# Packing the first segment's score visits into 512 columns, in a kernel whose instruction order is a searched list

## The chip, the cores and the metric

The kernel runs on one core of one Trainium2 chip. The metric is the device time of one execution in microseconds, from the program's start to its end; lower is better. Five engines work side by side, each in its own order of instructions: TensorE (PE, with PEld for its weight loads), VectorE (DVE), ScalarE (ACT), GpSimd (POOL) and SyncE (SP, which here only issues DMAs). They wait for each other through semaphores.

## The reference, cut to what matters

A pre-norm transformer block in bf16: 2048 tokens, 640 columns, 32 heads of 20. The attention is Infini-attention, over 4 segments of 512 tokens, with a memory (M, z) carried from segment to segment. The MLP has 1728 hidden columns.

```python
def _A_ref(x, wq, wk, wv, wo, beta):          # B=1, S=2048, H=32, Dh=20, N=4 segments, L=512
    ...                                       # q, k, v = x @ w, split into heads and segments
    phi = lambda t: jnp.where(t > 0, t + 1.0, jnp.exp(t))
    g = sigmoid(beta)
    for s in range(N):
        logits = jnp.einsum('bhqd,bhkd->bhqk', qs, ks) * scale + mask     # causal
        a_dot = softmax(logits) @ vs
        num, den = phi(qs) @ M, phi(qs) @ z + 1e-06
        o = g * num / den + (1.0 - g) * a_dot
        M, z = M + phi(ks).T @ vs, z + phi(ks).sum()
    return o @ wo
h  = x + _A_ref(layernorm(x), wq, wk, wv, wo, beta)
h2 = h + silu(layernorm(h) @ w1) @ w2
```

## The kernel before, in words

**Order.** Every piece of work is a task with a name. A string, `ORDER`, lists all tasks in the order in which they are recorded; each engine runs its own tasks in that order. The part of a row behind `:` gives the buffers (PSUM banks among them), the part behind `/` another engine than the task's first choice (`/A` ScalarE, `/D` VectorE, `/G` GpSimd). `fillN` are N matmuls on zeroes, put where TensorE is expected to have nothing else.

**Front of a segment** (`declare_front`). Blocks of 128 tokens are normalised: statistics (`n1_st`, DVE), the reciprocal root (`n1_r`, POOL, its first step in some blocks on DVE), the scaling (`n1_ap`, DVE, into `xn_rot`). The result is turned to columns by a DMA transpose (`n1_tr`, on SP's queue) in segments 1 to 3. In segment 0 TensorE turns it (`n1_tp`, line 750) and one copy of 640 columns a block brings it from PSUM to `hT` (`n1_te`, lines 759 and 760). The weights wq and wk are loaded raw into `sT` and rearranged by copies (`re_wq`, `re_wk`) into five chunks of 128 columns: each chunk holds four heads in strips of 32 partitions, 20 rows a head; the 12 rows left over hold pieces of the last 12 heads. Projections (`pr`, line 826) make q (w=0) and k (w=1) of chunk c; in segment 0 each is made in two halves of 256 tokens, x and y (`pr040x`: segment 0, chunk 4, q, first half), and copied out by `qe`. `v` (line 793) makes v, copied out by `ve`.

**The gathered tile.** The last 12 heads' q and k are put together from the left-over rows by 12 DMAs (`vt`, line 845, on SP's queue), into three more chunks, groups 5, 6 and 7. Before them the tile is zeroed by one memset (`vz0` for segment 0, `vz1` for the tile of the later segments, line 847). In segment 0 these tiles lie in the memory of w2 (`w_sb` in the profile).

**Score visits** (`scores`). For a group g of four heads, `qk` (line 912) makes the causal score blocks, keys on partitions and queries on columns, into four PSUM banks, one a head; two ScalarE instructions (`e`, line 923) take the exponential of two banks each into a slot of `PT`; POOL zeroes the upper triangle of each diagonal block (`mk`, line 934). In segment 0 a group has three visits: `x`, queries 0 to 255, 384 columns (256 for key block 0, 128 for key block 1); `ya`, queries 256 to 511 with key blocks 0 and 1, 512 columns; `yb`, the same queries with key blocks 2 and 3, 384 columns.

**Tick** (`tick`). `av` (line 955) multiplies by v, `oe` (lines 968, 970) copies out, `tn` turns the result back, `nm` normalises it into `otok`. `kt`, `mz`, `ma`, `mb` make the memory: `kt` is a DMA transpose of phi(k).

**Back** (`declare_back`). `ot` turns `otok` by a DMA transpose on SP's queue, `wo` (line 1124) multiplies by wo, `rs` adds the input; `n2_...` normalises and turns again by DMA; `h1` (line 1159), `th`, `s` are the first MLP product with the silu, `h2` (line 1201) the second, `o` and `out` the result. The MLP of one segment is spread between the score visits of the next.

`warm` (line 588) is a tanh of zeroes, 1280 wide, that writes two spare rows of `w2_sb` before the last rows of w2 are loaded over half of each.

Of the kernel before, what the change touches and what calls it, by code (L numbers as in the profile page):

```python
# [324 lines left out]
D = 640  # L325
# [3 lines left out]
L = 512  # L329
# [24 lines left out]
epsc:0 zpad x0:0 iota sel halfc x1:1 w_q:0 vz1:0 n1_st0:5 x2:2,3 n1_st1:3 n1_r0 n1_r1/D warm:0 n1_ap0:0 n1_ap1:1  # L354
fill29:7 n1_tp0:0 n1_te0:0 re_wq2:0 re_wq3 n1_st2:7 fill3:2 n1_tp1:2 w_k n1_r2 n1_te1 n1_st3:0 re_wq0/A fill8:4
pr020x:4 re_wq1/A re_wk0:0 pr030x:5 re_wq4 re_wk1/A mt0 n1_ap2:2 pr000x:6 re_wk2 pr010x:7 n1_r3 n1_ap3:3 pr001x:0
qe000x:0 re_wk3 pr011x:1 qe020x:0 n1_tp2:2 x8:4,5,6,10 qe010x:0 n1_tp3:6 qe030x/D:0 re_wk4/A pr021x:4 qe011x n1_te2
qe001x/D pr041x:5 beta qe021x/D x4:7,8,9,11 n1_te3/D w_w1_0:0 n1_st9:1 w_w1_2 qk0x0:0 lsc0 qe041x:0 e0x0:0 e0x2
pr040x:4 pr031x:5 w_wv:0 n1_st7:3 pr041y:6 vz0/G:0 qk1x0:0 n1_r7 qe040x qe041y e1x2:1 lsc1 pr030y:7 pr040y:4 pr031y:6
qe031x/D e1x0 qe040y mk0x_0 w_w1_4 qe031y qk2x0:0 n1_st6:2 e2x2:2 qe030y/D pr011y:5 n1_st4:4 e2x0 pr001y:4 pr000y:7  # L360
n1_r4/D mk1x_0 qk3x0:0 mk2x_0 pr021y:6 qe000y/D qe021y/D vpad1 pr010y:7 n1_st5:6 qe001y/D mk2x_256 e3x2:3 e3x0 qe011y
n1_ap7:0 pr020y:2 vt04 vt08 v00:0 mk1x_256 qe020y vt01 qe010y ex011:0 ex031:1 vpad0 lsc2 qk4x0:2 ve00/D:0 vt011 e4x0:6
n1_r6/D pha011:0 vt05 n1_st8:5 v01:6 mk0x_256 vt02 e4x2 qk0yb0:0 vt06 mta0 ve01/D zf0 phb011 v03:4 pha001:1 mk3x_0
vt03 vt00 n1_r5/D lsc3 pha031:2 ex001:2 mtb0 e0yb0:4 e0yb2 n1_ap4:1 vt07 vt09 n1_ap6:2 av0x:6 av2x:7 n1_r9/D mk4x_0
vt010 n1_ap5:3 qk1yb0:0 ve03 mk3x_256 phb031 v02:4 e1yb2:5 oe0x/D:0 e1yb0 oe2x/D:1 mk4x_256 qk7x0:0 ve02/D e7x2:0 e7x0
n1_tr4:0 tn0x:6 mm1 mm6 n1_tr5 av1x:7 kt01:0 oe1x/D:0 n1_tr6 qk5x0:2 w_w1_3 tn1x:7 av3x:0 e5x0:2 nm0x:0,0 nm1x:1 e5x2
oe3x/D:0 mk7x_0 mk7x_256 tn2x:6 fill3:1 qk6x0:0 av4x:7 av7x:4 e6x2:1 nm2x:2 v11:5 pha051:0 e6x0 oe7x/D:1 phb001 ve11:1
mk0yb_0 n1_tr7 mk6x_0 mk6x_256 tn7x:3 v10:0 mk5x_0 ex051:0 ex021:1 oe4x/D:1 qk0ya0:4 mk5x_256 e0ya0:3 tn3x:2 mk0yb_256
# [35 lines left out]
s0_1_1 pr230:6 th0_0_1:1 s0_0_1 e16e0:4 qe230 ad14 tn15:0 e16e2 mk16b_0 h1_0_10_1:7 h1_0_12_1:2 h1_0_5_1:3 pha200:0
kt16:0 th0_10_1:0 ex220:1 nm15:3,0 ad15 mz16:6 pha201:0 ex200:0 kt17:1 vt210:0 h1_0_6_1:4 ot6:0 s0_10_1 th0_12_1:1 ot7
ex201:2 v22:0 th0_6_1:0 s0_12_1 pha220:0 h1_0_11_1:5 th0_5_1:1 mk16a_0 h1_0_2_1:7 s0_6_1 mz17 ve22 ot4 out1/A s0_5_1
vt22 th0_11_1:0 th0_2_1:1 ot5 qk17b0:0 s0_11_1 e17b0:5 ma13 phb201 s0_2_1 vt28 kt20:1 ex211:2 wo6:4 h1_0_9_1:6 e17b2
mk16b_384 h1_0_3_1:7 mk16e_0 vt25 pha221:2 phb220 rs6 vt21 pha211:1 qk18b0:0 vt27 wo7:4 th0_3_1:0 mk16e_256 e18b0:0
th0_9_1:1 n2_st6:6 e18b2 vt20 phb200 vt23 s0_3_1 av16:0 n2_r6 pha230:0 rs7 ex230:1 ex221:0 s0_9_1 h1_0_13_1:1 qk17a0:2
oe16/D:1 th0_13_1:0 e17a2:1 wo4:6 mk17b_0 e17a0 s0_13_1 phb211 mk17b_384 h2_2_0:0 phb221 rs4 n2_st4:0 qk18e0:4 wo5:2  # L410
# [50 lines left out]
def build(nc, es, A_x, A_wq, A_wk, A_wv, A_wo, A_beta, B_x, B_w1, B_w2, out):  # L461
# [815 lines left out]
```

## Time and profile before

| | |
|---|---|
| time of the runs, median (lowest to highest) | 303.35 us (302.07 to 304.94), 3 runs |
| the profiled execution's own time | 302.65 us |
| its span in the profile | 300.9 us |
| granted TensorE clock | 1.00 throughout |
| PE busy | 288.7 us, 96% |
| DVE busy | 234.4 us, 78% |
| ACT busy | 230.5 us, 77% |
| POOL busy | 135.8 us, 45% |

Busy shares are means over stages with different limits. PE's end times are modelled, with pipelined matmuls laid over each other, so that a busy PE may still lose time in short steps; what ends a stage is seen in the waits of that stage. A row of the timeline gives the start, the length, the engine, the line, what is written and read, how many instructions were merged, and in brackets the engine's idle time just before with what ended it.

### The profile page before, as it was taken

Reading aid. Unit: us, or ns where it says so; the run is one execution under the profiler, and the core shown is the slowest. Engines: PE = TensorE matmul, PEld = TensorE weight load, DVE = VectorE, ACT = ScalarE, POOL = GpSimd, SP = SyncE. Lnnn points to the kernel's source line nnn. Section 1 sums busy time; section 2 is a strip of 40 time slices with the busy share of each in tenths; the row PEclk is TensorE's granted clock in tenths of the full one; section 3 lists DMA queues with packets and bytes.
Section 4 is the critical chain, followed back from the end, with each engine's and each line's share of the span. In section 5 each row is a group of like instructions: output and inputs, shape, how many; then the busy total and the mean of one; then the engine's idle time right before and its main releaser. Section 6 shows DMA issues by size and latency. Waiting matters only on the chain.

```text
span 300.9 us, 7531 instructions
## 1 busy us (share of the span) xinstructions
PE 288.7 (96%) x2994; PEld 169.5 (56%) x2994; DVE 234.4 (78%) x553; ACT 230.5 (77%) x337; POOL 135.8 (45%) x246
## 2 busy tenths in 40 slices
PE   8899888999999999989999899999999999999996
PEld 6675545555555455666643445556564457764575
DVE  6989887878798979879899976967868687835523
ACT  3889898999999999989889979998999741004500
POOL 2537843544566664445746715465395640200000
DMA  7953595556535320253662330233161004130002
GB/s 259 332 183 61 122 202 121 124 144 116 96 72 103 74 59 1 37 119 63 99 164 47 35 68 2 45 70 59 20 89 46 0 2 109 38 96 24 22 22 89
DMA packets 53603, 25.85 MB, mean 86 GB/s; under 512 B 44032, under 2 KB 52480, under 8 KB 53568
## 3 DMA queue, kind: packets, MB, share of 16 engines
q1 hardware_dynamic: 52144, 23.81, 36.5%
q10 hardware_dynamic: 1424, 1.56, 1.5%
q8 instruction: 24, 0.39, 0.6%
q14 instruction: 11, 0.09, 0.1%
HBM read 10.41 MB, written 2.62 MB: 43 GB/s over the span
## 4 chain that ended last, share of the span: by engine, by line
PE 66%; ACT 13%; DVE 12%; DMA 5%; issue 2%; POOL 1%
PE ps_all L1201 18%; PE ps_all L1159 15%; PE ps_all L826 10%; ACT PT L923 9%; PE ps_all L1124 7%; PE ps_all L912 6%; PE ps_all L955 5%; PE ps_all L793 3%; DMA oT<-otok 3%; DVE xn_rot L741 2%; DVE stt L719 2%; DVE oTs L970 1%; DMA xT<-xn_rot 1%; ACT th L1168 1%; ACT ex L866 1%
## 5 line engine op out<-in xcount | busy, mean ns | idle before, releaser
L923 ACT ACTIVATE PT<-ps_all 128x1024 bf16<-128x1024 f32 (+1 forms) x168 | 156.8, 987 | 10.0 <-PE ps_all L912 9.1
L934 POOL TENSOR_SCALAR_AFFINE_SELECT PT<-PT 128x512 bf16<-128x512 bf16 x128 | 80.8, 651 | 55.7 <-ACT PT L923 54.8
L1201 PE MATMUL ps_all<-w_sb,sT 128*128 128x320 bf16 (+2 forms) x462 | 65.5, 295 | 0.0
L1159 PE MATMUL ps_all<-hT,w_sb 128*128 128x512 bf16 (+1 forms) x325 | 63.3, 337 | 0.4 <-DVE otok L1003 0.2
L1168 ACT ACTIVATE th<-ps_all 128x512 f32<-128x512 f32 (+1 forms) x70 | 34.1, 509 | 34.6 <-PE ps_all L1159 27.0
L1201 PEld LDWEIGHTS ps_all<-w_sb,sT 128*128 128x128 bf16 x462 | 43.1, 98 | 19.0 <-issue 1.9
L1174 DVE SCALAR_TENSOR_TENSOR sT<-th,ps_all 128x512 bf16<-128x512 f32 (+2 forms) x70 | 38.0, 560 | 16.9 <-ACT th L1168 16.4
L1159 PEld LDWEIGHTS ps_all<-hT,w_sb 128*128 128x128 bf16 x325 | 29.3, 98 | 24.1 <-issue 3.2
L735 POOL TENSOR_TENSOR rst<-rst,eps_c 128x1 f32<-128x1 f32 x32 | 19.9, 623 | 23.7 <-DVE rst L729 22.3
L719 DVE BATCH_NORM_STATS2 stt<-x_tok 128x6 f32<-128x320 bf16 x64 | 27.9, 477 | 0.8 <-DMA x_tok<-in_A_x_dram 0.6
L1029 POOL TENSOR_TENSOR otok<-on 128x320 bf16<-128x320 bf16 x24 | 19.0, 797 | 17.8 <-DVE on L1021 17.8
L1124 PE MATMUL ps_all<-wo_sb,oT 128*128 128x320 bf16 x160 | 24.1, 300 | 1.9 <-DMA oT<-otok 1.6
L1214 DVE SCALAR_TENSOR_TENSOR x_tok<-ps_all,x_tok 128x640 bf16<-128x640 f32 (+3 forms) x18 | 13.3, 745 | 14.1 <-PE ps_all L1201 13.8
L955 PE MATMUL ps_all<-PT,Vx 128*32 128x256 bf16 (+3 forms) x576 | 23.7, 287 | 0.5 <-ACT PT L923 0.2
L970 DVE TENSOR_SCALAR oTs<-ps_all,lsc 128x512 bf16<-128x512 f32 (+1 forms) x33 | 20.3, 622 | 1.8 <-PE ps_all L955 1.1
L1021 DVE TENSOR_TENSOR on<-ps_all,rd 128x640 bf16<-128x640 f32 x24 | 19.8, 824 | 0.8
L1124 PEld LDWEIGHTS ps_all<-wo_sb,oT 128*128 128x128 bf16 x160 | 14.7, 98 | 9.7 <-issue 2.4
L741 DVE TENSOR_SCALAR xn_rot<-x_tok,mvt,rst 128x640 bf16<-128x640 bf16 x32 | 18.1, 572 | 2.2 <-POOL rst L735 2.1
L793 PE MATMUL ps_all<-wv_sb,xT 128*128 128x320 bf16 x120 | 18.2, 300 | 1.3 <-DMA xT<-xn_rot 1.0
L826 PE MATMUL ps_all<-xT,wqr 128*128 128x512 bf16 x75 | 18.7, 380 | 0.6 <-issue 0.6
L826 PE MATMUL ps_all<-xT,wkr 128*128 128x512 bf16 x75 | 18.7, 380 | 0.3 <-ACT PT L923 0.3
L1132 DVE TENSOR_TENSOR x_tok<-ps_all,x_tok 128x640 bf16<-128x640 f32 x16 | 13.1, 818 | 7.1 <-PE ps_all L1124 7.0
(90 smaller groups left out, 364.2 us busy)
## 6 DMA issues: line engine op xcount, KB each, us to landing
w_sb<-in_B_w_dram SPq DMA_DIRECT2D x5, 432.0 KB, 10.1
x_tok<-in_A_x_dram SPq DMA_DIRECT2D x3, 640.0 KB, 8.6
w_sb<-in_B_w_dram SPq DMA_DIRECT2D x3, 480.0 KB, 4.7
out_dram<-x_tok SPq DMA_DIRECT2D x9, 160.0 KB, 1.9
out_dram<-x_tok ACTq DMA_DIRECT2D x6, 160.0 KB, 1.8
QKV<-QK SPq DMA_DIRECT2D x12, 72.0 KB
sT<-in_A_wq_dram SPq DMA_DIRECT2D x1, 800.0 KB, 5.8
sT<-in_A_wk_dram SPq DMA_DIRECT2D x1, 800.0 KB, 7.4
```

The costliest lines, as they stand in the source:

```text
L719: T.add(DV, lambda e, hh=hh: e.bn_stats(out=stt[:, s, 6 * hh:6 * hh + 6], in_=xb[:, 320 * hh:320 * hh + 320]), reads=R((xa, xsub)), writes ...
L741: T.add(eng, lambda e: e.tensor_scalar(out=xn_rot[:, xn.slot, :], in0=x_tok[:, b % 12, :], scalar1=mvt[:, s, 0:1], scalar2=rst[:, s, :], o ...
L793: fns.append(lambda e, c=c, hh=hh: e.matmul(bank(ps, hh)[:, 0:320], lhsT=xT_[:, c, 128 * i:128 * i + 128], rhs=wv_sb[:, c, 320 * hh:320 * ...
L826: fns = [lambda e, kc=kc: e.matmul(bank(ps)[:, lo:hi], lhsT=wt[:, kc, c, :], rhs=xT_[:, kc, lo:hi], start=(kc == 0), stop=(kc == NC - 1)) ...
L923: T.add(AC, lambda e: e.activation(out=pt[:, pta.slot, q0:q0 + 2, 0:width], in_=sc3[:, b0:b0 + 2, 0:width], func=ACT.Exp, scale=SCALE), re ...
L934: T.add(PO, lambda e: e.affine_select(out=v, in_=v, pattern=[[0, 4], [1, 128]], compare_op=ALU.is_ge, fill=0.0, base=0, channel_multiplier ...
L955: fns.append(lambda e, j=j, r=r, h=h, pa=pa, pt=pt, co=co, q0=q0, ji=ji: e.matmul(bank(po)[32 * r:32 * r + 32, q0:hi], lhsT=Vx[:, vx.slot, ...
L1124: fns.append(lambda e, c=c, hh=hh: e.matmul(bank(ps, hh)[:, 0:320], lhsT=oT[:, c, 128 * i:128 * i + 128], rhs=wo_sb[:, c, 320 * hh:320 * h ...
L1159: fns = [lambda e, c=c: e.matmul(bank(ps)[:, lo:hi], lhsT=w1_sb[:, c, 128 * f:128 * f + 128], rhs=hT[:, c, lo:hi], start=(c == 0), stop=(c ...
L1168: T.add(AC, lambda e: e.activation(out=th[:, tha.slot, lo:hi], in_=bank(ps)[:, lo:hi], func=ACT.Tanh, scale=0.5), reads=R((ps, [0])), writ ...
L1174: T.add(DV, lambda e: e.scalar_tensor_tensor(out=sT[:, f, lo:hi], in0=th[:, tha.slot, lo:hi], scalar=1.0, in1=bank(ps)[:, lo:hi], op0=ALU. ...
L1201: fns.append(lambda e, f=f, t0=t0, fr=fr, hh=hh, n=n: e.matmul(bank(pa, hh)[:, 0:n], lhsT=sT[:, f, t0:t0 + 128], rhs=w2_sb[:, fr, c0 + 320 ...
```

## The change

It has four parts.

- **Packing** (`declare_ticks`, segment 0). The x visits of groups 4 to 7 become three of 512 columns: `4p` (group 4 whole, and group 6's second key block), `5p` (group 5 and group 7's second key block), `6w` (the first key blocks of 6 and 7). The yb visits of groups 0 to 3 become `0r`, `1r`, `2s` in the same way, those of 4 to 7 `4r`, `5r`, `6s`. The x visits of groups 0 to 3 and all ya visits stay. `PT` gets 8 slots for 7.
- **Finer pieces at the start.** The copy of a turned block is split into 384 and 256 columns (`n1_te0a`, `n1_te0b`); the first half of q is projected and copied in two blocks of 128 tokens (`u` and `v` for `x`). Dependences follow these pieces (`XS`, `WH`).
- **Zeroing.** `vz` can only be on VectorE; `vz0` was on POOL.
- **The list.** `ORDER` is a new one from first row to last, made by a search that assumed each DMA transpose to land late.

```diff
-SPLIT0 = tuple((c, w) for c in range(5) for w in range(2))
-WH = [(0, 0), (0, 1), (1, 0), (1, 1)]
+WH = [(0, 0), (0, 2), (0, 1), (1, 0), (1, 2), (1, 1)]
+def XS(b0, b1):
+    return [10 * k + b for b in range(b0, b1) for k in range(2)]
...
-    PT = sb("PT", [128, 7, 4, 512], BF16)
+    PT = sb("PT", [128, 8, 4, 512], BF16)
...
-                src = ps_all[:, 512 * ps.slot:512 * ps.slot + 640].rearrange("p (c t) -> p c t", c=NC)
+            for k, (c0, c1) in enumerate(((0, 3), (3, NC))):
...
-                for hh, (b0, b1) in enumerate([(0, 2), (2, 4)] if s == 0 and (c, w) in SPLIT0 else [(0, 4)]):
+                for hh, (b0, b1) in enumerate(([(0, 1), (1, 2), (2, 4)] if w == 0 else [(0, 2), (2, 4)]) if s == 0 else [(0, 4)]):
...
-            G.task(f"vz{s}", {DV: 0.9, PO: 3.0}, lambda eng: ...
+            G.task(f"vz{s}", {DV: 0.9}, lambda eng: ...
...
+                hx = [(0, 0), (0, 2), (1, 0), (1, 2)]
+                pa = scores(f"{g0}p", "PT", PT, [(g0, 0, 0, 256, 0), (g0, 1, 128, 256, 256), (g2, 1, 128, 256, 384)], k, sub=hx)
+                pb = scores(f"{g1}p", "PT", PT, [(g1, 0, 0, 256, 0), (g1, 1, 128, 256, 256), (g3, 1, 128, 256, 384)], k, sub=hx)
+                pc = scores(f"{g2}w", "PT", PT, [(g2, 0, 0, 256, 0), (g3, 0, 0, 256, 256)], k, sub=hx)
...
+                pa = scores(f"{g0}r", "PT", PT, [(g0, 2, 256, 512, 0), (g0, 3, 384, 512, 256), (g2, 3, 384, 512, 384)], k)
+                pb = scores(f"{g1}r", "PT", PT, [(g1, 2, 256, 512, 0), (g1, 3, 384, 512, 256), (g3, 3, 384, 512, 384)], k)
+                pc = scores(f"{g2}s", "PT", PT, [(g2, 2, 256, 512, 0), (g3, 2, 256, 512, 256)], k)
```

The first place is the start of POOL's list. `w_sb` of 3072 is the gathered tile of segment 0, `Vx` the tile of v whose spare columns are set once, `rst` the reciprocal root of a block. Before, from the third block's root on:

```order
L732 TENSOR_TENSOR rst<-mvt,eps_c 128x1
L735 TENSOR_TENSOR rst<-rst,eps_c 128x1
L847 MEMSET w_sb 128x3072
L732 TENSOR_TENSOR rst<-mvt,eps_c 128x1
L735 TENSOR_TENSOR rst<-rst,eps_c 128x1
```

Now, on VectorE from its first instruction:

```order
L589 MEMSET zpad 128x128
L851 MEMSET w_sb 128x1536
L624 TENSOR_SCALAR ident<-iot 128x128
L722 BN_STATS stt<-x_tok 128x6 x2
L725 BN_AGGR mvt<-stt 128x2
```

The zeroing has left POOL, where it stood behind the roots of the first four blocks, and stands on VectorE ahead of the first block's statistics, where `vz1` stood; `vz1` now comes behind the first ticks of segment 0. POOL sets `Vx` at its start, and not among the masks.

The second place is ScalarE in segment 0, where the exponentials of the first half end (in the first row those of `1yb`, `7x`, `5x` and `6x`) and those of the second half go on. `PT` of 2x384 is half of a 384-column visit, `PT` of 1024 half of a 512-column one; `ex` belongs to phi(k). Before:

```order
L923 ACTIVATE PT<-ps_all 128x2x384 x8
L803 ACTIVATE Vx<-ps_all 128x32x20
L866 ACTIVATE ex<-w_sb 128x512 x2
L923 ACTIVATE PT<-ps_all 128x1024 x3
L968 ACTIVATE oTs<-ps_all,lsc 128x256
L923 ACTIVATE PT<-ps_all 128x1024
L923 ACTIVATE PT<-ps_all 128x2x384 x2
```

Now, from the first packed visit to `warm`:

```order
L927 ACTIVATE PT<-ps_all 128x1024 x6
L870 ACTIVATE ex<-w_sb 128x512
L927 ACTIVATE PT<-ps_all 128x1024 x4
L870 ACTIVATE ex<-w_sb 128x512
L927 ACTIVATE PT<-ps_all 128x1024 x2
L807 ACTIVATE Vx<-ps_all 128x32x20
L972 ACTIVATE oTs<-ps_all,lsc 128x256 x3
L927 ACTIVATE PT<-ps_all 128x1024
L1107 ACTIVATE Mz<-ps_all 128x168
L927 ACTIVATE PT<-ps_all 128x1024 x3
L870 ACTIVATE ex<-w_sb 128x512
L927 ACTIVATE PT<-ps_all 128x1024 x2
L591 ACTIVATE w_sb<-zpad 128x1280
```

All exponentials after group 3's are 1024 wide: two of the yb kind (`0r`, `1r`) come first, then `4p`, `5p`, `6w`. The last row is `warm`, which was ScalarE's first instruction and now stands between the visits.

The third place is TensorE at the end of segment 1's attention, from the turning of its last group (`tn15`, with `oTs`) to the first output projection (`wo6`, with `wo_sb`), which needs the DMA transpose of `otok`. Before:

```order
L984 MATMUL ps_all<-Mzb,phiQ 128x84 x4
L988 MATMUL ps_all<-ident,oTs 128x84 x4
L1159 MATMUL ps_all<-hT,w_sb 128x256 x15
L1077 MATMUL ps_all<-Vx,phiKt 128x84 x4
L1159 MATMUL ps_all<-hT,w_sb 128x256 x5
L793 MATMUL ps_all<-wv_sb,xT 128x320 x10
L1159 MATMUL ps_all<-hT,w_sb 128x256 x10
L1077 MATMUL ps_all<-Vx,phiKt 128x84 x4
L912 MATMUL ps_all<-QK 128x384 x4
L912 MATMUL ps_all<-QK 128x128 x4
L1124 MATMUL ps_all<-wo_sb,oT 128x320 x10
```

Now:

```order
L988 MATMUL ps_all<-Mzb,phiQ 128x84 x4
L992 MATMUL ps_all<-ident,oTs 128x84 x4
L1178 MATMUL ps_all<-hT,w_sb 128x256 x15
L797 MATMUL ps_all<-wv_sb,xT 128x320 x10
L1096 MATMUL ps_all<-Vx,phiKt 128x84 x4
L1178 MATMUL ps_all<-hT,w_sb 128x256 x10
L1096 MATMUL ps_all<-Vx,phiKt 128x84 x4
L1178 MATMUL ps_all<-hT,w_sb 128x256 x10
L830 MATMUL ps_all<-xT,wqr 128x512 x5
L916 MATMUL ps_all<-QK 128x384 x4
L916 MATMUL ps_all<-QK 128x128 x4
L1143 MATMUL ps_all<-wo_sb,oT 128x320 x10
```

One more piece of the MLP (5 matmuls of 256) and one projection (5 of 512) stand between the last group's end and the output projection that waits for its transpose.

More of the change, by code (lines that the diff above doesn't have):

```diff
@@ L353 @@
 ORDER = """
[L354 to L368, printed above, removed]
@@ L404 @@
[L404 to L408, printed above, removed]
@@ L861, in declare_front @@
                 exa = G.alloc("ex")
-                src = (qk[c], [(w, 0), (w, 1)]) if c < 5 else (qv, list(range(12)))
+                src = (qk[c], [(w, 0), (w, 1), (w, 2)]) if c < 5 else (qv, list(range(12)))
                 iv = QK_[:, c, w, :] if c < 5 else QKV_[:, c - 5, w, :]
```

247 lines of the change are left out of this document (138 added, 109 removed), and 2 rows, old and new, of the table pools.

## The prediction

> **What bounds the kernel now.** I read the stages first (start, length, then busy us of PE, PEld, DVE, ACT and POOL, PEclk, DMA share, GB/s), then the timeline where a stage loses time, then the chain.
>
> ```profile
> 7.00:16.00 9.00, 7.55 (x83) 6.20 (x82) 8.90 (x28) 6.43 (x19) 4.50 (x6) 1.00 0.93 343
> 16.00:31.00 15.00, 14.74 (x164) 9.95 (x162) 13.67 (x42) 14.46 (x27) 9.60 (x20) 1.00 0.39 98
> 31.00:48.00 17.00, 14.52 (x206) 7.76 (x205) 13.37 (x39) 14.43 (x20) 9.24 (x18) 1.00 0.88 162
> 48.00:100.00 52.00, 50.56 (x636) 28.63 (x634) 44.30 (x118) 51.29 (x73) 26.92 (x58) 1.00 0.53 111
> 100.00:130.00 30.00, 29.51 (x327) 17.03 (x320) 26.13 (x58) 29.75 (x46) 17.46 (x27) 1.00 0.19 37
> 130.00:180.00 50.00, 47.77 (x480) 25.63 (x479) 44.01 (x103) 44.66 (x63) 25.08 (x46) 1.00 0.47 88
> 180.00:245.00 65.00, 64.60 (x707) 35.78 (x706) 49.75 (x104) 57.21 (x76) 37.06 (x57) 1.00 0.21 39
> 245.00:301.00 56.00, 53.52 (x382) 34.30 (x380) 29.71 (x57) 9.76 (x18) 3.97 (x7) 1.00 0.20 54
> ```
>
> From 16 to 31 us and from 48 to 130 ScalarE is busy 95.50 of 97 us: there it sets the pace, with TensorE close behind. From 130 us TensorE does. The stages with slack on both are the start (ACT 6.43 of 9.00) and 31 to 48 (ACT idle 17 - 14.43 = 2.57 us, PE 2.48). So a change earns where it starts ScalarE's stream sooner, fills 31 to 48, shortens ScalarE's own work up to 130 us, or takes a wait from TensorE after that. The clock is 1.00 in every stage and plays no part.
>
> **The start.** Start, length, engine, line, what, count, and in brackets the idle time before:
>
> ```profile
> 1.12 6.08 PE L607 MATMUL ps_all<-zpad 128*128 128x256 bf16 x29 [1.12 <-DVE zpad L586]
> 7.52 1.31 ACT L759 ACTIVATE hT<-ps_all 128x640 bf16<-128x640 f32 x2 [3.21 <-PE ps_all L750]
> 9.89 0.37 DVE L685 COPY wkr<-sT 128x400 bf16<-128x400 bf16 x2
> 10.16 0.82 ACT L683 ACTIVATE wkr<-sT 128x400 bf16<-128x400 bf16 x2
> 10.59 0.42 DVE L741 TENSOR_SCALAR xn_rot<-x_tok,mvt,rst 128x640 bf16<-128x640 bf16 x1
> 10.91 2.87 POOL L847 MEMSET w_sb<- 128x3072 bf16 x1
> 10.94 2.90 DVE L685 COPY wkr<-sT 128x400 bf16<-128x400 bf16 x2
> 11.32 2.68 DVE L741 TENSOR_SCALAR xn_rot<-x_tok,mvt,rst 128x640 bf16<-128x640 bf16 x1
> 14.06 0.45 PE L750 MATMUL ps_all<-ident,xn_rot 128*128 128x128 bf16 x5 [1.45 <-DVE xn_rot L741]
> 15.64 0.38 ACT L834 ACTIVATE w_sb<-ps_all 128x256 bf16<-128x256 f32 x1 [2.05 <-PE ps_all L826]
> 15.94 1.51 ACT L923 ACTIVATE PT<-ps_all 128x768 bf16<-128x768 f32 x2
> ```
>
> While POOL zeroes the gathered tile (10.91 to 13.78), two copies that took 0.37 us a moment earlier take 2.90, and the scaling of the fourth block ends at 14.00 in place of about 10.94 + 0.37 + 0.42 = 11.7. TensorE then waits 1.45 us and ScalarE 2.05. With the memset on VectorE this stall of some 2.3 us goes. The trace has the other memset there:
>
> ```profile
> 1.70 1.34 DVE L847 MEMSET QKV<- 128x1536 uint32 x1 [0.27 <-issue]
> 3.66 0.89 DVE L719 BATCH_NORM_STATS2 stt<-x_tok 128x6 f32<-128x320 bf16 x2 [0.62 <-DMA x_tok<-in_A_x_dram]
> 24.30 1.18 DVE L741 TENSOR_SCALAR xn_rot<-x_tok,mvt,rst 128x640 bf16<-128x640 bf16 x1
> 24.59 0.67 POOL L614 MEMSET Vx<- 128x128 bf16 x1
> 24.83 0.46 POOL L615 MEMSET Vx<- 128x48 bf16 x1
> ```
>
> It takes 1.34 us before x has landed, so `vz0` costs nothing in that place. What is new is that POOL sets `Vx` beside it, 2 x (0.67 + 0.46) = 2.26 us; no row shows a VectorE memset beside a POOL one. Its price lies between nothing and a delay of the first statistics by some 0.3 us (both run after each other, from 0.97 to about 4.0); I take nothing, as the nearest pair that did not stall is VectorE's statistics beside POOL. At 24.30 such a memset held a scaling, 1.18 for 0.42; that pair goes too, but under a busy ScalarE it is worth nothing. [...]
>
> Late next is ScalarE itself. From its first copy to the first exponential it takes 15.94 - 7.52 = 8.42 us, of which it waits 2.05: 6.4 of work. After the change that work is: one rearrangement fewer (0.82 from the row at 10.16), one copy of 256 columns fewer, eight of 128 more, three block copies in two pieces each, `lsc0` gone behind the exponential.
>
> ```profile
> 23.39 0.99 ACT L834 ACTIVATE w_sb<-ps_all 128x256 bf16<-128x256 f32 x3
> 31.50 4.50 ACT L923 ACTIVATE PT<-ps_all 128x768 bf16<-128x768 f32 x6 [0.54 <-PE ps_all L912]
> 43.24 1.51 ACT L923 ACTIVATE PT<-ps_all 128x768 bf16<-128x768 f32 x2 [0.55 <-PE ps_all L912]
> 47.95 3.77 ACT L923 ACTIVATE PT<-ps_all 128x1024 bf16<-128x1024 f32 x4 [0.68 <-PE ps_all L912]
> ```
>
> A copy of 256 costs 0.33 back to back; 128 columns is not in the trace, between 0 and 0.33; on the line through 768 columns (4.50 / 6 = 0.75) and 256 it is 0.33 - 128 x 0.42 / 512 = 0.22, which I take. Split block copies add a fixed part each, at most 0.2 by the same line (0.33 - 256 x 0.42 / 512 = 0.12), so 0.4 for three. Sum: -0.8 - 0.3 + 8 x 0.22 + 0.4 - 0.2 = +0.9, so 7.3 us of work. Four fill matmuls fewer (6.08 / 29 = 0.21 each) let it start up to 0.6 earlier, at about 6.9. Without any wait the first exponential would start at 14.2, 1.7 before the old 15.94; with all of the old wait it would start later, at 16.3. The waits for wk and for TensorE do not all go: I take **-1.0**, ends +0.3 and -1.7. The 25 matmuls more of half width stream the same columns and cost nothing.
>
> **31 to 48 us.** Here ScalarE waits 0.54, 0.55 and 0.68 us in the three rows above for score matmuls. The first is the gather, the last follows the output projection waiting for its transpose:
>
> ```profile
> 20.15 8.92 SPq L845 DMA_DIRECT2D w_sb<-w_sb  x12
> 46.04 1.53 PE L1124 MATMUL ps_all<-wo_sb,oT 128*128 128x320 bf16 x10 [0.75 <-DMA oT<-otok]
> 132.37 1.53 PE L1124 MATMUL ps_all<-wo_sb,oT 128*128 128x320 bf16 x10 [0.83 <-DMA oT<-otok]
> 173.24 1.53 PE L793 MATMUL ps_all<-wv_sb,xT 128*128 128x320 bf16 x10 [1.03 <-DMA xT<-xn_rot]
> ```
>
> The 12 gather DMAs are issued from 20.15 to 29.07, once q and k are copied out. The new list copies chunks 3 and 4 first and issues their eight DMAs first, so the gather should end with the earlier start, one or two us sooner. At the first `wo`, one v projection (1.53 us by the row) stands in front that stood behind: more than the 0.75. I take half of the 2.57 us as won: **-1.3**, ends 0 (other waits come) and -2.57. `vz1` now lies here on VectorE, 1.34 us by its row at the start; VectorE has 17 - 13.37 = 3.6 us free in this stage, which covers it. Were it not covered, v's last block would be late by 1.34.
>
> **ScalarE's work in the visits.** Packing takes 24 exponentials of 768 and adds 18 of 1024. By the rows that is 24 x 0.75 = 18.0 against 18 x 3.77 / 4 = 17.0: **-1.0**. The elements are the same; six fixed parts go. [...] Against it stands `warm`:
>
> ```profile
> 3.04 1.27 ACT L588 ACTIVATE w_sb<-zpad 128x1280 bf16<-128x1280 bf16 x1
> 59.57 0.55 PE ps_all L1159 x5
> 61.10 1.08 PE ps_all L826 x5
> ```
>
> It was at 3.04 us, where ScalarE had nothing; now it stands between exponentials in the paced stage: **+1.3**. The DMA of w2's last rows waits for it, with the turning of the normalised h behind that on SP; the MLP's first product hangs on those.
>
> **TensorE after 130 us.** It waited 0.83 and 1.03 us for transposes (rows above). At the first, 0.55 + 1.08 = 1.63 us of matmuls (the two rows of the chain just quoted) stand in front of `wo6` that did not. At the second, `v32` in segment 3, the new list has the v projection of another block (1.53 by the row) and a score visit more between the scaling of its block and its use. Both waits should go: -1.9; as a list new from first to last makes waits of its own, I take **-1.5**, ends -1.9 and +1.5 (as many new as now).
>
> **Sum.** -1.0 - 1.3 - 1.0 + 1.3 - 1.5 = -3.5. The profiled execution took 302.65 us, 1.75 beyond its span of 300.9; 302.65 - 3.5 = 299.15. The median of the runs is 0.70 above that execution, so in its terms 303.35 - 3.5 = **299.8**. About 1% either way (3 us) is what a measurement of this kernel can tell from no change: the runs before spread from 302.07 to 304.94.
>
> **Rivals**, in terms of the median.
>
> *The gains reach the end in full*: start -1.7, stage 31 to 48 -2.6, transposes -1.9, ScalarE as above +0.3: -5.9, 297.4. For it: TensorE has no other long wait after 16 us. Against: it needs a new list without a new wait.
>
> *The gather decides* (the change doesn't do what it says). All packed visits of groups 4 to 7 need the gathered tile; before, `4x` did not, and seven visits of two exponentials stood in front of the first that did (14 x 0.75 = 10.5 us); now four of these and two of the wide kind (8 x 0.75 + 4 x 0.94 = 9.8), so 0.7 us of cover is gone. If the last DMA still lands near 31 us, ScalarE, which comes 1.0 us sooner by the start and 0.7 by the visits, waits 2.2 in place of 0.54; both first terms are lost: 302.1. Eight fill matmuls that now stand before `6w` speak for it, the earlier DMAs against.
>
> *Slower: ScalarE pays.* `warm` (+1.3) and the copies (+0.9) lie in ScalarE's stream; if the start is bound by that stream, its term is +0.3, and if the idle 2.57 us stays, packing's -1.0 is all there is against 1.3. With as many new transposes' waits as old ones, +1.5: 0.3 + 0.3 + 1.5 = +2.1, 305.5. It decides from the point where ScalarE has under 0.5 us idle between 16 and 48 us without being earlier. The paced 48 to 130 us speak for it; the 2.05 and 2.57 idle us against.
>
> **How the numbers follow.** Forecast (298 to 301) 0.45; in full (294.5 to 298) 0.22; gather (301 to 304) 0.20; slower (304 to 308) 0.13. Faster by over 1% is below 300.3: all of the second and three quarters of the first, 0.56; slower by over 1%, above 306.4, is 0.07; within 1% the other 0.37. The range from 294.5 to 305.0 leaves out most of the slower case.
>
> **What would show it.** Right: no VectorE instruction above 1.5 us near 11 us; the first exponential before 15.3; ScalarE idle under 1.5 us in the 17 us after its first 15 of exponentials; no wait of TensorE over 0.5 us for `oT` or `xT`; `warm` at 1.27 us between exponentials. Wrong: a wait of ScalarE over 1 us at the first packed visits of groups 4 to 6; TensorE waiting for `hT` at the first MLP product; the DMA waits after 130 us back in other places.

## The result and the profile after

The changed kernel took 299.98 us in the median (299.36 to 301.19, 4 runs) beside 303.38 (302.07 to 304.94) for the kernel before: ratio 0.988, 95% interval 0.983 to 0.992. The profiled execution took 300.29 us with a span of 298.6 (before 302.65 and 300.9). Measured twice more, on two chips, the ratio was 0.989 (0.984 to 0.994) and 0.9935 (0.991 to 0.996).

One thing is needed to read these numbers and those of the experiments: in some executions of every kernel here TensorE's mean granted clock is 0.994 or less, and they are 0.8 to 2.3 us longer (medians of each kernel; the last section shows what happens in them), so beside each median over all runs I give the median of the executions whose mean granted clock is 0.999 or more ("at full clock").

The stages after, with the same columns as those shown of before:

```profile
7.00:16.00 9.00, 8.47 (x111) 7.00 (x110) 8.67 (x35) 8.32 (x30) 2.57 (x9) 1.00 0.99 357
16.00:31.00 15.00, 13.39 (x170) 9.17 (x168) 12.91 (x35) 14.72 (x26) 9.16 (x20) 1.00 0.42 85
31.00:48.00 17.00, 16.23 (x210) 9.29 (x209) 13.49 (x34) 16.34 (x23) 10.36 (x21) 1.00 0.81 143
48.00:100.00 52.00, 49.97 (x628) 28.79 (x626) 45.22 (x118) 51.24 (x71) 24.43 (x49) 1.00 0.55 117
...
130.00:180.00 50.00, 49.88 (x492) 25.70 (x491) 44.21 (x105) 47.47 (x65) 24.01 (x43) 1.00 0.44 80
```

ScalarE, the fourth of the busy columns, is busy 8.32 us in the first stage where it had 6.43, and idles 0.66 us from 31 to 48 us where it had 2.57. TensorE, the first, is busy 49.88 of 50 us from 130 to 180 us where it had 47.77. By this table ScalarE or TensorE is busier in every stage in which the prediction looked for a gain. The timeline of the start and of the stage from 28 to 48 us:

```profile
1.32 1.34 DVE L851 MEMSET w_sb<- 128x1536 uint32 x1 [0.27 <-issue]
...
1.56 0.82 POOL L617 MEMSET Vx<- 128x128 bf16 x1
...
9.93 1.56 ACT L838 ACTIVATE w_sb<-ps_all 128x128 bf16<-128x128 f32 x7
...
11.13 0.79 DVE L744 TENSOR_SCALAR xn_rot<-x_tok,mvt,rst 128x640 bf16<-128x640 bf16 x2
...
14.73 0.85 ACT L927 ACTIVATE PT<-ps_all 128x768 bf16<-128x768 f32 x1
...
17.68 8.85 SPq L849 DMA_DIRECT2D w_sb<-w_sb  x12
...
28.95 0.40 PE L916 MATMUL ps_all<-w_sb 20*128 20x256 bf16 x12 [0.94 <-DVE Vx L808]
...
29.40 1.94 ACT L927 ACTIVATE PT<-ps_all 128x1024 bf16<-128x1024 f32 x2 [0.22 <-PE ps_all L916]
...
46.00 1.53 PE L1143 MATMUL ps_all<-wo_sb,oT 128*128 128x320 bf16 x10 [0.35 <-DMA oT<-otok]
...
46.18 1.33 ACT L591 ACTIVATE w_sb<-zpad 128x1280 bf16<-128x1280 bf16 x1
...
47.91 1.94 ACT L927 ACTIVATE PT<-ps_all 128x1024 bf16<-128x1024 f32 x2 [0.40 <-PE ps_all L916]
```

The zeroing takes 1.34 us on VectorE beside GpSimd's `Vx` memsets, as it did without them; two scalings take 0.79 us near 11 us, where one took 2.68; the first exponential starts at 14.73 (before 15.94); the gather is issued until 26.53 (before 29.07). `warm` stands between exponentials. All that TensorE waits for from 100 us to 260 us, in the view of its waits (in total, times, longest), is

```profile
PE ps_all L1143 <- DVE rd L1019: 0.4, 1, 0.4
PE ps_all L988 <- ACT oTs L972: 0.3, 1, 0.3
PE ps_all L916 <- ACT PT L927: 0.2, 1, 0.2
```

and no transpose is among it.

### The profile page after: what moved, and what is told of

Same layout as the page of the kernel before. It is cut to its first block, busy times and chain, and to the rows that moved or that the text cites. A ratio compares the mean times of both kernels' runs of the same rounds, so it can differ in the third digit from the quotient of the medians.

```text
span 298.6 us, 7582 instructions
## 1 busy us (share of the span) xinstructions
PE 288.3 (97%) x3018; PEld 169.5 (57%) x3018; DVE 233.2 (78%) x549; ACT 229.5 (77%) x339; POOL 134.4 (45%) x251
## 3 DMA queue, kind: packets, MB, share of 16 engines
q10 hardware_dynamic: 1568, 1.56, 1.5%
## 4 chain that ended last, share of the span: by engine, by line
PE 69%; DVE 11%; ACT 9%; SPq 4%; DMA 4%; issue 2%; POOL 1%; DVEq 0%; ACTq 0%
PE ps_all L1178 19%; PE ps_all L1220 17%; PE ps_all L830 10%; ACT PT L927 7%; PE ps_all L916 6%; PE ps_all L959 5%; PE ps_all L1143 4%; PE ps_all L797 4%; SPq L849 2%; DVE stt L722 2%; SPq L1135 2%; DMA oT<-otok 2%; PE ps_all L992 1%; PE ps_all L988 1%; DVE xn_rot L744 1%
## 5 line engine op out<-in xcount | busy, mean ns | idle before, releaser
L1193 DVE SCALAR_TENSOR_TENSOR sT<-th,ps_all 128x512 bf16<-128x512 f32 (+1 forms) x70 | 37.8, 558 | 16.3 <-ACT th L1187 15.8
L738 POOL TENSOR_TENSOR rst<-rst,eps_c 128x1 f32<-128x1 f32 x32 | 18.6, 580 | 19.4 <-DVE rst L732 17.6
L974 DVE TENSOR_SCALAR oTs<-ps_all,lsc 128x512 bf16<-128x512 f32 (+1 forms) x31 | 19.7, 641 | 1.7 <-PE ps_all L992 0.8
L1143 PEld LDWEIGHTS ps_all<-wo_sb,oT 128*128 128x128 bf16 x160 | 14.7, 97 | 9.0 <-issue 3.2
L735 POOL TENSOR_TENSOR rst<-mvt,eps_c 128x1 f32<-128x1 f32 x23 | 5.0, 217 | 32.7 <-DVE mvt L725 32.7
L839 DVE CAST QK<-ps_all 128x512 bf16<-128x512 f32 x23 | 15.7, 686 | 5.0 <-PE ps_all L830 4.8
```

The source lines that it names most:

```text
L1143: fns.append(lambda e, c=c, hh=hh: e.matmul(bank(ps, hh)[:, 0:320], lhsT=oT[:, c, 128 * i:128 * i + 128], rhs=wo_sb[:, c, 320 * hh:320 * h ...
L1193: T.add(DV, lambda e: e.scalar_tensor_tensor(out=sT[:, f, lo:hi], in0=th[:, tha.slot, lo:hi], scalar=1.0, in1=bank(ps)[:, lo:hi], op0=ALU. ...
```

## The experiments

All were timed against the kernel before on the same chip. Medians in us; "full clock" with the number of executions that had it.

| kernel | median, runs | full clock | ratio to before (95%) |
|---|---|---|---|
| before, chip 1 / 2 / 3 | 303.22, 23 / 302.67, 26 / 302.94, 23 | 302.56 (14) / 302.44 (21) / 302.76 (18) | |
| changed, first measurement | 299.98, 4 | 299.67 (3) | 0.988 (0.983 to 0.992) |
| `a_again`, chip 1 | 299.89, 6 | 299.84 (5) | 0.989 (0.984 to 0.994) |
| `a_again2`, chip 3 | 301.06, 9 | 299.60 (2) | 0.9935 (0.991 to 0.996) |
| `a_pool_zero`, chip 1 | 303.23, 12 | 302.19 (3) | 0.999 (0.996 to 1.002) |
| `a_pool_pieces`, chip 2 | 302.30, 12 | 302.14 (8) | 1.000 (0.998 to 1.002) |
| `a_pool_start`, chip 3 | 300.71, 10 | 299.87 (5) | 0.9925 (0.990 to 0.9955) |
| `b_dve_zero`, chip 2 | 300.48, 6 | 300.49 (6) | 0.9935 (0.991 to 0.996) |
| `b_dve_zero2`, chip 3 | 300.28, 10 | 300.16 (8) | 0.993 (0.991 to 0.996) |
| `a_warm_first`, chip 1 | 300.51, 6 | 299.42 (3) | 0.9895 (0.985 to 0.994) |
| `a_warm2`, chip 3 | 300.93, 7 | 299.78 (2) | 0.9935 (0.991 to 0.996) |
| `a_split_exp`, chip 1 | 300.84, 12 | 300.35 (7) | 0.993 (0.989 to 0.996) |
| `a_whole_q`, chip 2 | 301.01, 12 | 300.38 (7) | 0.997 (0.994 to 0.9995) |
| `b_late_use`, chip 2 | 303.52, 9 | 303.29 (6) | 1.005 (1.003 to 1.0075) |

### The zeroing put back on GpSimd

```diff
-            G.task(f"vz{s}", {DV: 0.9}, ...
+            G.task(f"vz{s}", {DV: 0.9, PO: 3.0}, ...
-iota:0 zpad epsc x1:0 vpad0 vz0:0 vpad1 ... n1_r2 re_wk3 n1_r3 w_w1_1:0
+iota:0 zpad epsc x1:0 vpad0 vpad1 ... n1_r2 re_wk3 n1_r3 vz0/G:0 w_w1_1:0
```

> The changed kernel with one part undone: the gathered tile of segment 0 is zeroed on GpSimd again, behind the first four roots, as in the kernel before; VectorE's place at the start stays empty. Theory (a GpSimd memset holds VectorE's copies, and the start feeds a paced stream): a VectorE instruction of over 2 us near 12 to 14 us, the first exponential 1.0 to 2.0 us later than at 14.73, and 1 to 2 us more at the end, 301.0 to 302.0. Rival (the start's gain is given back before the first output projection, which came at 46.0 us in both kernels): the same stall at the start, and less than 0.5 us at the end.

The start of `a_pool_zero` in the timeline:

```profile
11.12 3.31 DVE L744 TENSOR_SCALAR xn_rot<-x_tok,mvt,rst 128x640 bf16<-128x640 bf16 x2
...
11.26 2.65 POOL L851 MEMSET w_sb<- 128x3072 bf16 x1
...
14.36 0.40 DVE L688 COPY wkr<-sT 128x400 bf16<-128x400 bf16 x2
...
15.91 0.49 ACT L763 ACTIVATE hT<-ps_all 128x384 bf16<-128x384 f32 x1 [3.06 <-DVE hT L764]
...
17.24 0.85 ACT L927 ACTIVATE PT<-ps_all 128x768 bf16<-128x768 f32 x1
```

The pair of scalings takes 3.31 us for 0.79, that is 2.52 more, ScalarE waits 3.06 us for VectorE's half of a block copy, and the first exponential comes 17.24 - 14.73 = 2.51 us later. At full clock the end is 302.19 - 299.84 = 2.35 us later. So the stall goes from the first exponential to the end nearly whole. The theory has the mechanism right and both sizes too low, 1.0 to 2.0 us at the first exponential and 1 to 2 us at the end; the rival falls. And with the zeroing back, all the rest of the change together stands at a ratio of 0.999 (0.996 to 1.002): over all runs no gain shows, and at full clock it is 302.56 - 302.19 = 0.4 us, by three executions.

### The zeroing alone moved in the kernel before

```diff
-epsc:0 zpad x0:0 iota sel halfc x1:1 w_q:0 vz1:0 n1_st0:5 ... pr041y:6 vz0/G:0 qk1x0:0 ... nm2x:2 v11:5
+epsc:0 zpad x0:0 iota sel halfc x1:1 w_q:0 vz0:0 n1_st0:5 ... pr041y:6 qk1x0:0 ... nm2x:2 vz1:0 v11:5
```

> The kernel before with one thing of the change: VectorE zeroes segment 0's gathered tile at the start of its own list, in the place of `vz1`, and `vz1` goes behind `nm2x`; no other row is moved. Theory A (the zeroing on VectorE is the gain, and it carries to the end whole): no copy and no xn_rot near 11 us takes over 1.5 us, the first exponential is about 2.5 us earlier than 15.94, and the median is 2.5 to 3.4 us below before, as much as putting it back cost the changed kernel. Theory B (it pays only beside the other edits): the earlier start is given back at the first group's waits of ScalarE on TensorE or at the gather, and the median is within 1.2 us of before.

> The kernel before with the zeroing of segment 0's gathered tile on VectorE at the start, beside the changed kernel on one chip; no other row is moved but `vz1`. Theory A: 2 to 2.6 us below before and within 0.6 us of the changed kernel. Theory B: 1 to 2 us below before, and 1.2 to 2.5 us above the changed kernel.

> The changed kernel as it is, beside the kernel before with the zeroing on VectorE alone, on one chip. Theory A (the zeroing is nearly all of the gain, and the packing, the finer copies and the searched list are worth nothing together): the two medians are within 0.6 us. Theory B (the rest is worth what the prediction put on it, 2.5 us for packing, middle and end): the changed kernel is 1.2 to 2.5 us below.

Rows of the kernel before, VectorE's sum with the residual behind the first output product of segment 0 and of segment 1:

```profile
47.61 0.82 DVE L1132 TENSOR_TENSOR x_tok<-ps_all,x_tok 128x640 bf16<-128x640 f32 x1 [1.46 <-PE ps_all L1124]
...
133.94 0.82 DVE L1132 TENSOR_TENSOR x_tok<-ps_all,x_tok 128x640 bf16<-128x640 f32 x1 [1.01 <-PE ps_all L1124]
```

The timeline of `b_dve_zero`, its start and the same two rows, and its wait at `v32`:

```profile
11.29 0.45 DVE L741 TENSOR_SCALAR xn_rot<-x_tok,mvt,rst 128x640 bf16<-128x640 bf16 x1
...
13.91 1.51 ACT L923 ACTIVATE PT<-ps_all 128x768 bf16<-128x768 f32 x2
...
45.19 0.82 DVE L1132 TENSOR_TENSOR x_tok<-ps_all,x_tok 128x640 bf16<-128x640 f32 x1 [1.32 <-PE ps_all L1124]
...
130.80 0.82 DVE L1132 TENSOR_TENSOR x_tok<-ps_all,x_tok 128x640 bf16<-128x640 f32 x1 [0.26 <-PE ps_all L1124]
...
170.00 1.53 PE L793 MATMUL ps_all<-wv_sb,xT 128*128 128x320 bf16 x10 [0.90 <-DMA xT<-xn_rot]
```

With the same list otherwise, everything moves together: the first exponential from 15.94 to 13.91 (-2.0), the residual sum at 47.61 by -2.4, that at 133.94 by -3.1, where the wait for the transpose at `wo6` has gone without any row being moved there, and the span by 300.9 - 297.7 = 3.2. Over all runs the gain is 0.0065 x 302.67 = 2.0 us (1.3 to 2.6) and 2.1 us on the third chip (at full clock 2.0 and 2.6), less than in the profiled execution, the fastest of six that lie between 299.41 and 301.08 us. So Theory A of the first text has the kind right and the sizes too high: it gave 2.5 us at the first exponential and 2.5 to 3.4 at the end.

On the third chip the changed kernel stands at 0.9935 and the one moved memset at 0.993. Over all runs the packing, the finer copies and the searched list add nothing to it (301.06 against 300.28); at full clock they are worth 300.16 - 299.60 = 0.6 us, by two executions on one side. The changed kernel's first two measurements, 0.988 and 0.989, leave room for about 1 us more, but there the moved memset alone was not timed. Theory A of the last two texts holds in kind, one memset moved having nearly all of the gain, though the medians over all runs are 0.8 us apart where it gave 0.6; the 1.2 to 2.5 us of theory B don't show.

### What a memset on GpSimd holds, and where it may stand

```diff
-                                      lambda eng: T.add(eng, lambda e: e.memset(QKV_[:, :, :, :], 0.0),
+                                      lambda eng: [T.add(eng, lambda e, p=p: e.memset(QKV_[:, p, :, :], 0.0),
+                                                   ...) for p in range(3)],
```

> The changed kernel with the zeroing of segment 0's gathered tile back on GpSimd where it stood before, but as three memsets of a third of the tile each. Theory A (an SBUF-to-SBUF instruction of VectorE is held until the memset running on GpSimd ends, so the length of one memset is what counts): the longest VectorE instruction near 11 us takes 0.9 to 1.4 us, and the median is 1 to 1.5 us above the changed kernel. Theory B (VectorE is held as long as GpSimd has memsets to run): one VectorE instruction takes 2.5 to 3 us as with one memset, or two or three take 1 us each, and the median is 3 us above the changed kernel.

`a_pool_pieces` differs from `a_pool_zero` by this alone. Its timeline:

```profile
11.13 3.21 DVE L744 TENSOR_SCALAR xn_rot<-x_tok,mvt,rst 128x640 bf16<-128x640 bf16 x2
...
11.26 2.90 POOL L851 MEMSET w_sb<- 128x1024 bf16 x3
...
14.26 0.40 DVE L688 COPY wkr<-sT 128x400 bf16<-128x400 bf16 x2
```

These rows put together two scalings and three memsets. In shorter windows they come apart:

```profile
11.13 2.14 DVE L744 TENSOR_SCALAR xn_rot<-x_tok,mvt,rst 128x640 bf16<-128x640 bf16 x1
...
11.26 1.83 POOL L851 MEMSET w_sb<- 128x1024 bf16 x2
...
13.04 1.12 POOL L851 MEMSET w_sb<- 128x1024 bf16 x1
...
13.19 1.15 DVE L744 TENSOR_SCALAR xn_rot<-x_tok,mvt,rst 128x640 bf16<-128x640 bf16 x1
...
13.33 0.45 PE L753 MATMUL ps_all<-ident,xn_rot 128*128 128x128 bf16 x5 [1.31 <-DVE xn_rot L744]
```

The first scaling is held through two memsets, not until the first ends, and is done at 13.27, when the third has just begun; TensorE turns its block at 13.33. The second scaling is held through the third memset. Together they take 3.21 us, nearly as with one memset (3.31), and the ratio is 1.000 (0.998 to 1.002), at full clock 2.3 to 2.5 us above the changed kernel on other chips. So theory B holds in what counts, and in neither of its forms exactly. Each scaling ends 0.18 us after a memset does, by these rows: at 13.27 after 11.26 + 1.83 = 13.09, and at 13.19 + 1.15 = 14.34 after 13.04 + 1.12 = 14.16.

The other kernel leaves the memset whole, on GpSimd, but early:

```diff
-iota:0 zpad epsc x1:0 vpad0 vz0:0 vpad1 halfc x0:1
+iota:0 zpad epsc x1:0 vpad0 vpad1 halfc vz0/G:0 x0:1
```

> The changed kernel with the zeroing of segment 0's gathered tile on GpSimd again, but at the start of its list, behind `halfc`, where VectorE has only the first two tiles' statistics to do (3.73 to 5.65 us) and no copy of weights. Theory A (what costs is the place: a copy or xn_rot of VectorE is held by a memset of GpSimd, statistics are not): the statistics of 320 elements start at 3.7 us and take 0.42 to 0.5 us each as in the changed kernel, the first exponential is within 0.3 us of 14.73, and the median is within 0.4 us of the changed kernel. Theory B (a long memset of GpSimd holds any VectorE instruction): the first statistics end after 5.0 us instead of 4.1, and all behind it, with the median 0.9 to 1.5 us above the changed kernel.

```profile
1.16 3.91 DVE L624 TENSOR_SCALAR ident<-iot 128x128 bf16<-128x128 int32 x1
...
2.21 2.78 POOL L851 MEMSET w_sb<- 128x3072 bf16 x1
...
3.77 1.30 DVE L722 BATCH_NORM_STATS2 stt<-x_tok 128x6 f32<-128x320 bf16 x2
...
15.18 0.86 ACT L927 ACTIVATE PT<-ps_all 128x768 bf16<-128x768 f32 x1
```

Here a small VectorE instruction that I had not thought of, the making of `ident` (0.16 us in the changed kernel), is held from 1.16 us, through the short `Vx` memsets and the long one, until the latter's end, and the first statistics end at 5.07 instead of 4.62. But VectorE had no x before 3.7 us anyway: the first exponential is 0.45 us later, and the time is the changed kernel's (299.87 against 299.60 at full clock, ratios 0.9925 and 0.9935). So theory A has the time, within its 0.4 us, but not the start (0.45 us for 0.3), and theory B has the late statistics, but not their price. The gain is not VectorE's faster memset (1.34 us against 2.78); it is the place.

### ScalarE's part: `warm`, the fixed parts, the finer copies

```diff
-x2:2,3 n1_ap0:0 n1_r1 n1_ap1:1 fill25:7 ... ve13/D warm:0 w_w1_2
+x2:2,3 n1_ap0:0 n1_r1 n1_ap1:1 warm:0 fill25:7 ... ve13/D w_w1_2
```

> The changed kernel with the tanh of zeroes (1280 wide) back in front of ScalarE's first copy, where it stood before; all else as in the changed kernel. Theory (ScalarE's stream sets the pace from 16 to 130 us, so that its 1.33 us there are paid): 1.0 to 1.3 us less, 298.7 to 299.0. Rival (it stands in front of a score visit that TensorE brings late anyway, and TensorE's list sets the end): within 0.4 us of 300.0, with a wait of ScalarE for score matmuls in its place.

> The changed kernel itself, once more, so that the edits of it beside it on the same chip have a reference. Every theory: about 300.0 us, 3.4 below the kernel before.

> The changed kernel with `warm` back at the front, the candidate for the fastest version, beside the changed kernel on one chip. Theory A (its 1.3 us of ScalarE in mid-stream reach the end in part): 0.3 to 0.7 us below the changed kernel. Theory B (ScalarE waits for TensorE's scores there anyway): within 0.2 us of it.

The timeline of `a_warm_first`:

```profile
44.38 1.98 ACT L927 ACTIVATE PT<-ps_all 128x1024 bf16<-128x1024 f32 x2
...
47.40 1.94 ACT L927 ACTIVATE PT<-ps_all 128x1024 bf16<-128x1024 f32 x2 [1.04 <-PE ps_all L916]
```

With `warm` gone from here, ScalarE's next exponential starts at 47.40 instead of 47.91 and waits 1.04 us for scores instead of 0.40: of 1.33 us, 0.51 is left on the spot. At the end it is 299.42 against 299.84 on one chip and 299.78 against 299.60 on another, ratios alike: nothing that these runs can tell. The rival of the first text and theory B of the last hold, and the candidate for a faster version is not one.

```diff
+                        cuts = [(0, 256), (256, 512)] if name[-1] in "pwrs" else [(0, width)]
+                        for w0, w1 in cuts:
...                          # one exponential of the two banks for each cut
```

> The changed kernel with each of the 18 exponentials of the packed visits made in two halves of 256 columns a bank: the same elements, 18 ScalarE instructions more, three times what packing removes in number. Theory (packing is worth six fixed parts of 0.17 to 0.2 us, since ScalarE paces): 18 x 0.17 = 3.1 us more at the end, 303.1. [...] Rival (ScalarE has slack where the packed visits stand): under 0.5 us.

Rows of the packed visits, one of the changed kernel and then two of `a_split_exp`:

```profile
25.41 3.77 ACT L927 ACTIVATE PT<-ps_all 128x1024 bf16<-128x1024 f32 x4
...
26.43 5.21 ACT L929 ACTIVATE PT<-ps_all 128x512 bf16<-128x512 f32 x10
...
32.20 4.03 ACT L929 ACTIVATE PT<-ps_all 128x512 bf16<-128x512 f32 x8
```

An instruction more costs (4.03 - 3.77) / 4 = 0.07 us in one row and (5.21 - 5 x 3.77 / 4) / 5 = 0.10 in the other, where I had taken (24 x 0.75 - 18 x 3.77 / 4) / 6 = 0.17. Eighteen of them cost 300.35 - 299.84 = 0.5 us at full clock, 0.95 over all runs: far less than the 3.1 of the theory, and nearest to the rival's 0.5. By that proportion packing's six are worth 0.2 to 0.3 us at the end, an estimate; a kernel with the packing alone undone was not timed.

```diff
-                for hh, (b0, b1) in enumerate(([(0, 1), (1, 2), (2, 4)] if w == 0 else [(0, 2), (2, 4)]) if s == 0 else [(0, 4)]):
+                for hh, (b0, b1) in enumerate([(0, 2), (2, 4)] if s == 0 else [(0, 4)]):
```

> The changed kernel with the first half of segment 0's queries of heads group 0 projected and copied as one block of 256 positions, as before, not as two of 128; the rest of the list as it stands. This undoes the finer copies alone. Theory A (the 128-wide copies, at 0.22 us for seven in 1.56 us on ScalarE, start the exponentials earlier and pay): first exponential 0.3 to 0.8 us later than 14.73 us and the median 0.3 to 0.8 us above the changed kernel. Theory B (they cost as many fixed parts as they save waiting): the median is within 0.3 us of the changed kernel, or below it.

The expectation's "queries of heads group 0" is too narrow: the first half of the queries is made whole for all five chunks. The turned blocks are still copied in two pieces. Its timeline on ScalarE:

```profile
11.65 0.94 ACT L837 ACTIVATE w_sb<-ps_all 128x256 bf16<-128x256 f32 x3 [1.64 <-PE ps_all L829]
...
15.16 0.81 ACT L926 ACTIVATE PT<-ps_all 128x768 bf16<-128x768 f32 x1
```

ScalarE waits 1.64 us for the first whole piece; the first exponential is 0.43 us later, and the full-clock median 0.5 to 0.8 above those of the changed kernel (300.38 against 299.60 to 299.84, on other chips), which fits theory A. The finer copies of the queries are the part of the rest for which a gain shows.

### The two waits of TensorE after 130 us

```diff
-wo6:4 h1_0_9_1:6 e17b2 mk16b_384 h1_0_3_1:7 mk16e_0 ... v32:2 n1_tr15 ... h1_1_10_0:4 ex251:0
+h1_0_9_1:6 e17b2 mk16b_384 h1_0_3_1:7 wo6:4 mk16e_0 ... n1_tr15 ... h1_1_10_0:4 v32:2 ex251:0
```

> The kernel before with two rows moved and nothing else: the first output product of the last two tiles, `wo6`, goes behind the first half of MLP tile 3, and the value product `v32` behind that of MLP tile 10. Theory A (after 130 us TensorE paces, as the prediction had it): the waits of 0.83 us at `wo6` and 1.03 us at `v32` go, no other takes their place, and the median is 1.5 to 2 us below before. Theory B (the two waits are slack of a stage that another engine paces): they go, and come back as other waits; the median is within 0.7 us of before.

```profile
137.82 1.38 PE L1124 MATMUL ps_all<-wo_sb,oT 128*128 128x320 bf16 x9 [0.68 <-DVE x_tok L1132]
...
178.65 0.40 PE L912 MATMUL ps_all<-QKV 20*128 20x512 bf16 x4 [0.89 <-ACT Vx L803]
```

(In the profiled execution the clock fell far ahead of these rows: its mean is 0.72 from 14 to 15 us and 0.50 from 15 to 17.) Both waits for a transpose after 130 us are gone, and there are two new ones of nearly their size: a later output product waits 0.68 us for VectorE to free a bank, and scores wait 0.89 us for ScalarE's copy of the late v. The kernel became slower, ratio 1.005 (1.003 to 1.0075), 0.85 us at full clock. Theory B has the mechanism, and the loss is above its 0.7 us. Which of the two moves lost the 0.85 us was not tried.

## Why the prediction was right, and where it was not

The number was met, 299.8 against 299.98, and so were the five signs: no VectorE instruction near 11 us over 0.79 us, first exponential at 14.73, ScalarE idle 0.66 us from 31 to 48 us, no wait for `oT` or `xT` over 0.35 us, `warm` at 1.33 us between exponentials. None of the three signs against it came. But the sum was right by terms whose errors cancel, and that it came within 0.2 us is luck: on the third chip the gain was 302.94 - 301.06 = 1.9 us over all runs.

- **Start, -1.0: mis-sized, 2.0 to 2.6.** Moving the memset alone gives 2.0 (1.3 to 2.6) in the old list over all runs, and 2.0 and 2.6 at full clock on two chips; undoing it costs 2.35 at full clock in the new one. The stall of "some 2.3 us" was read rightly from the rows, and for the first exponential itself the forecast was close: 15.94 to 14.73, -1.2. What failed was the next step, in which the stall was exchanged for ScalarE's own chain up to its first exponential, as if the 0.9 us of copies put ahead of it were lost at the end too. The first exponential of `b_dve_zero` is 0.8 us earlier than the changed kernel's (13.91 against 14.73), and its end is not earlier (300.16 against 299.60 on one chip at full clock). A start is to be measured at equal work, not at one instruction that now has more in front of it; how much of those copies stood behind it before was not counted. That the 25 matmuls more of half width cost about nothing holds: in the changed kernel, from 8 to 24 us, 50 of 128 columns are busy 3.5 us and 25 of 256 columns 3.4.
- **31 to 48 us, -1.3; packing, -1.0; `warm`, +1.3; TensorE after 130 us, -1.5: -2.5 together, measured about -0.6 at full clock, and -0.4 or nothing without the moved memset.** `warm` cost nothing that shows, since ScalarE waits for scores there (1.04 us in `a_warm_first`). Packing's -1.0 is time of ScalarE's by the rows, not time at the end, where 0.2 to 0.3 us is the estimate from `a_split_exp`; and the step from 768 to 1024 columns was read as a step in fixed parts of 0.17 us, where an instruction more measures 0.07 to 0.10 us (`a_split_exp`). ScalarE's idle time from 31 to 48 us did go, from 2.57 to 0.66 us, but it is no measure of a gain: with the moved memset alone ScalarE is busy 15.22 us there (14.43 before), and 16.34 - 15.70 = 0.6 us of the rest is `warm` itself, by `a_warm_first`.
- **TensorE after 130 us** was the step least founded. The first of its two waits goes by the earlier start alone (`b_dve_zero`), and moving both uses to a later place makes the old list slower. TensorE shows 49.88 of 50 us busy in that stage now, and the end is hardly earlier for it.
- **"The clock is 1.00 in every stage and plays no part"** held for the profiled execution, not for all; see below.

Of the rivals, "the gains reach the end in full" (297.4) was not reached. "Slower: ScalarE pays" put +1.3 on `warm` as the forecast did, and falls with it. "The gather decides" falls by the rows: the wait at the first packed visits is 0.22 us.

## What to carry to other kernels

When a VectorE instruction takes several times its usual length (here 2.90 us for 0.37), look for a GpSimd instruction that runs at the same moment, and move that to where VectorE has nothing to do; on which engine it then runs (299.87 us against 299.60), or in how many pieces (3.21 us of scalings against 3.31), mattered less here. A stall at the start, ahead of an engine that is busy from there on, was worth nearly its full length (2.35 of 2.52 us); a wait in the middle of a tuned list was worth little here (0.83 and 1.03 us went, 0.68 and 0.89 came), so look first at the engine behind it. Before a large change is credited with a gain, do its smallest part alone.

## What the runs showed of the hardware

TensorE's clock, from 27 us on, in an execution of the changed kernel with a mean granted clock of 0.994 (`a_again2`; PEclk is the third column from the end):

```profile
27.00:30.50 3.50, 1.94 (x49) 1.08 (x51) 3.47 (x10) 3.29 (x4) 2.73 (x5) 0.98 0.68 123
30.50:33.50 3.00, 3.00 (x18) 1.35 (x13) 2.10 (x4) 1.91 (x3) 1.54 (x3) 0.50 0.48 101
33.50:36.50 3.00, 2.73 (x42) 1.57 (x42) 1.73 (x4) 2.38 (x3) 2.02 (x5) 0.95 0.70 125
```

Then the timeline at that place in `a_again2`:

```profile
30.82 2.85 PE L797 MATMUL ps_all<-wv_sb,hT 128*128 128x320 bf16 x10
```

And the same row in `a_again`, which kept 1.00 there:

```profile
30.11 1.53 PE L797 MATMUL ps_all<-wv_sb,hT 128*128 128x320 bf16 x10
```

After a stretch in which TensorE is busy 1.94 of 3.50 us, the hole around the 0.94 us wait for a bank, the clock is 0.50 for 3.4 us, and ten products take 2.85 us for 1.53. The executions at 0.994 end at 301.1 us in the median (`a_again2`), those at full clock at 299.6. In the stretch ahead of the fall TensorE was idle for 1.56 us of the 3.50, in pieces, the longest of 0.94.

The hole alone does not decide. In `a_again` TensorE is busy 1.93 us in the same 3.50 us, and the clock stays at 1.00. In `a_pool_zero` it is busy 1.85 of the 3 us from 13 us on and the clock stays at 1.00; it is busy 1.76 of the 3 us from 30 us on, and from 33 to 34 us the clock is 0.53. What decides between such cases these traces don't show.

Whether an execution is hit varies: 19 of 72 of the kernel before, 9 of 19 of the changed one (7 of 9 on the third chip, 2 of 10 elsewhere), 9 of 12 with the memset back, 2 of 16 with the moved memset alone, whose TensorE is busy 2.77 of 3.50 us in that stretch. The place varies too. In `b_late_use` and `a_pool_pieces` the fall came near 14.4 and 14.7 us (mean clock 0.74 and 0.78 from 13 to 16 us), as the memset's stall ended, around which TensorE is busy 0.88 of the 3 us from 12 us on in the one and waits 1.31 us for a scaling in the other: the stall is itself such a hole. So the executions with a fall end some 1.5 us later in `a_again2`, and part of what the changed kernel won it gives back that way. That the hole is the cause was not tried: a kernel with matmuls on zeroes in it would show it.
